# A fused attention and soft mixture of experts on one core: other positions of all tasks, buffers given to expert tiles step by step, and the end laid out anew

## The chip, the core and the metric

The kernel runs on one core of a Trainium2 chip. The time is that of the device in microseconds for one execution; the median of several executions is given. Five engines work side by side, each on its own list of instructions: the tensor engine (PE, with its weight loads as PEld), the vector engine (DVE), the scalar engine (ACT), GpSimd (POOL) and SyncE (SP), which issues nearly all transfers.

## The reference

Attention over 8 images, 8 heads, 576 positions and 64 dimensions, then a soft mixture of 8 experts with 4 slots each (32 slots) over all 4608 rows of 512 features:

```python
q_rot, k_rot = rotate(q), rotate(k)
scores = scale * q_rot @ k_rot.T
attn = softmax(scores, -1)                 # per head, 576 x 576
x = (attn @ v).transpose(0, 2, 1, 3).reshape(4608, 512)
logits = x @ phi                           # 4608 x 32
d = softmax(logits, 0)                     # dispatch: over all rows
slot_input = (d.T @ x).reshape(8, 4, 512)
for e in range(8):
    slot_out[e] = relu(slot_input[e] @ w1[e]) @ w2[e]     # 512 -> 1024 -> 512
c = softmax(logits, 1)                     # combine: over the slots
out = c @ slot_out
```

## The kernel before

**Pairs.** Two heads of an image are a pair; there are 32 (NPAIR), four to an image. For each pair some forty small tasks run: load0 and load1 (q and k come in, two buffers x_in), spin0 and spin1 (rotation products on POOL), join (sum on DVE), high (float16 high half on ACT) and low (the rest, DVE), which together fill a buffer hl of the pool stk, four of them; eight tasks m00 to m31 and m_rem (scores once, in high halves, for each column's maximum, read by DVE from PSUM); m_min, m_turn, m_half and m_rows (the maxima are reduced, transposed, scaled, and sent by two small transfers into one of two tiles called peak); t0 to t8 (scores in three products and the peaks as a fourth, exponential by ACT into a_t, for t8 into a_rem); av0 to av8 (times v, all into one PSUM tile o_ps); o_out (ACT copies o_ps out in two pieces), recip, norm (POOL), natural (transpose on PE), natural_out (ACT), logits and logits_sum.

**Images.** After an image's last pair come stat0, stat1, slots (running maximum and sums over the rows, with rescaling) and soft0 to soft3 (softmax over the slots, the combine weights cn_sb).

**The order.** PE, ACT and DVE run in the order in which the program writes its tasks; SP and POOL too until the last pair is through. That order is the table WHEN (for pairs 0 to 4 the table FIRST): each task has a position in quarter pairs, to which 4 is added per pair, and `line` is all of them sorted (L590, run at L619). PSUM has three two-bank tiles (bank2, L210) for all tasks but av, which take turns.

**Expert weights.** They are 64 tiles of 512 KB. The first 26 (N_W) are loaded in the course of the pairs into the pool wp (task weights). When the last low is done, the input buffers are closed (release_io) and 7 tiles go there, one per task trickle0 to trickle3; after the last t8 the four hl buffers are closed (release_stk) for 4 more; after the last av8 those of attention (release_att) for one. Two (N_WB) come when the normed outputs xn are read, 7 (N_LEAD) and the remaining 17 when expert products have read the tiles of wp. SP issues them in this order.

**The end** (L627 to L835). Norm, transpose, logits and statistics of the last pair; the slot sums of the last image (mains, L670) and their rescaling (L695 to L714); the experts' first layer in four groups (ffn1, L720), each followed by a transpose (ffn1_turn); the second layer in 16 steps for each half of the features (ffn2_steps); gather; and nine combine tasks for each half, each with an output of 512 KB (L767). The second half's second layer is interleaved with the first half's combine. The combine weights are split in a high and low part (c_split), transposed on PE (c_tr) and copied out (c_evac), for two images at a time: turn 0 between the slot sums and their rescaling (L685), turn 1 after the first ffn1 (L793), turn 2 after the fourth, turn 3 in the first half's combine. An output is staged in one of seven tiles that held weights.

Of the kernel before, what the change touches and what calls it, by code (L numbers as in the profile page):

```python
# [28 lines left out]
N_W = 26  # L29
N_WA = 5  # L30
N_WB = 2
N_WE = 3
N_WL = 1
N_X = 4
N_CS = 1
N_CE = 2
C_POOL = 4
LATE = (0, 2)
N_LEAD = 7
TURNS = (0, 0, 1, 0, 0, 0)  # L40
LEAD_STEPS = 2
STEPS = (1, 2, 2, 2, 2, 2, 2, 2, 1)
N_WARM = 23
N_HEAT = 12
N_CST = 4 - N_CE
# [13 lines left out]
    "m_min": (-2.33553, -2.33553, -3.36903, -2.33553), "m_turn": (-1.87097, -1.91584, -1.95052, -1.87097),  # L59
    "m_half": (-1.83711, -1.83711, -1.79, -1.83711), "m_rows": (-0.49269, -0.26643, -0.62853, -0.47686),  # L60
# [56 lines left out]
def attn_softmoe(ctx, tc, qk, v, phi, w, cs, ident, sel, seg, out):  # L117
# [50 lines left out]

    loaded = {}
    halves = {}  # L170
    c_tiles = []
# [636 lines left out]
    for k in range(16):  # L808
# [3 lines left out]
        if k == 8:  # L812
            c_turns(TURNS[3])
# [77 lines left out]
```

## Time and profile before

| | us |
|---|---|
| median of 3 runs | 552.83 (552.35 to 553.71) |
| the profiled execution | 551.77 |
| its span, from the first to the last instruction | 550.0 |
| PE busy in it | 516.9 |
| DVE, ACT, POOL busy | 374.6, 308.5, 287.4 |
| mean granted clock of PE, share of 2.4 GHz | 0.974 |

The profile is of one execution. Busy times of PE include the modelled ends of pipelined matmuls. In a chain of waits each piece is what released the next, followed back from the last instruction; in a timeline each line is a run of like instructions, with its start, its length and, in brackets, the idle time before it.

### The profile page before, as it was taken

What the parts mean: (1) busy time and instruction counts of PE and PEld (TensorE: products, weight loads), DVE (VectorE), ACT (ScalarE), POOL (GpSimd) and SP (SyncE); (2) the same over time, 40 slices, a digit from 0 to 9 for tenths busy, and PEclk for the clock granted to TensorE, in tenths of its full rate; (3) what the DMA queues carried; (4) which work ended last, traced back from release to release, by engine and by line L of the source; (5) the groups of instructions that cost most, each with busy time, mean ns of one, the idle gap of its engine ahead of it and who ended that gap; (6) DMA issues with size and microseconds to landing.
All of it is one profiled execution on the core that took longest, in us unless ns stands there. A gap on an engine that the chain in (4) does not pass through costs nothing.

```text
span 550.0 us, 24116 instructions
## 1 busy us (share of the span) xinstructions
PE 516.9 (94%) x10824; PEld 388.4 (71%) x10824; DVE 374.6 (68%) x591; ACT 308.5 (56%) x615; POOL 287.4 (52%) x338
## 2 busy tenths in 40 slices
PE   4599999999999999999999999999999999799992
PEld 2277777777777777777777777777777777553551
DVE  6788768778777878787778777877887651222162
ACT  2156564766665666566656666566666656334442
POOL 3965678756665666565656766665767011110000
PEclk9699999999999999999999999999999999969997
DMA  7631554444435443544444353434343155349998
GB/s 244 199 125 35 198 190 151 134 145 160 148 108 190 151 143 123 183 158 114 150 151 167 100 179 107 170 119 159 125 151 114 34 212 203 107 133 398 409 415 330
DMA packets 28487, 93.92 MB, mean 171 GB/s; under 512 B 4064, under 2 KB 5856, under 8 KB 28384
## 3 DMA queue, kind: packets, MB, share of 16 engines
q1 hardware_dynamic: 28370, 92.37, 48.1%
q8 instruction: 85, 1.39, 1.0%
q14 instruction: 18, 0.15, 0.1%
q10 hardware_dynamic: 14, 0.00, 0.0%
HBM read 82.85 MB, written 9.44 MB: 168 GB/s over the span
## 4 chain that ended last, share of the span: by engine, by line
PE 83%; DVE 6%; DMA 5%; ACT 2%; issue 1%; SPq 0%; ACTq 0%; DVEq 0%
PE o_ps L303 27%; PE s_ps L268 22%; PE s_ps L221 9%; PE s_ps L350 4%; PE o_ps L310 4%; DMA w_exp<-in_w 3%; PE s_ps L229 2%; PE s_ps L272 2%; PE s_ps L724 2%; PE s_ps L410 1%; PE t_ps L775 1%; DVE nm L223 1%; PE s_ps L360 1%; PE s_ps L242 1%; DMA x_in<-in_qk 1%
## 5 line engine op out<-in xcount | busy, mean ns | idle before, releaser
L187 POOL TENSOR_TENSOR x_in<-x_in,cs_sb 128x288 f32<-128x288 f32 x248 | 221.8, 929 | 78.7 <-DMA x_in<-in_qk 65.9
L223 DVE TENSOR_REDUCE nm<-s_ps 128x2 f32<-128x576 f32 x256 | 188.3, 755 | 79.0 <-PE s_ps L221 74.8
L283 ACT ACTIVATE a_t<-s_ps 128x576 f32<-128x576 f32 x256 | 152.8, 653 | 126.1 <-PE s_ps L268 123.3
L303 PE MATMUL o_ps<-v_in,a_t 128*64 128x65 f32 x4608 | 164.5, 225 | 0.3 <-ACT o_sb L324 0.2
L303 PEld LDWEIGHTS o_ps<-v_in,a_t 128*64 128x64 f32 x4608 | 145.8, 138 | 25.3 <-issue 17.4
L268 PE MATMUL s_ps<-hl 64*128 64x288 f16 x1536 | 134.4, 283 | 0.6 <-DVE nm L231 0.3
L334 POOL TENSOR_TENSOR xn<-o_sb,rr 128x512 f32<-128x512 f32 x31 | 44.4, 1432 | 95.8 <-DVE rr L330 85.4
L268 PEld LDWEIGHTS <-hl 64*128 64x128 f16 x1536 | 76.1, 94 | 19.8 <-issue 2.3
L221 PE MATMUL s_ps<-hl 64*128 64x288 f16 x512 | 73.9, 291 | 3.6 <-DVE l_sb L372 1.4
L268 PE MATMUL s_ps<-peak,lift 64*128 64x288 f16 x512 | 74.5, 283 | 0.0
L191 DVE TENSOR_TENSOR x_in<-x_in 128x1152 f32<-128x1152 f32 (+1 forms) x35 | 50.8, 1451 | 0.1
L196 ACT CAST hl<-x_in 128x576 f16<-128x576 f32 (+1 forms) x66 | 40.6, 651 | 17.8 <-DVE x_in L191 17.7
L200 DVE TENSOR_TENSOR hl<-x_in,hl 128x1152 f16<-128x1152 f32 x32 | 43.3, 1355 | 0.4 <-ACT hl L196 0.4
L221 PEld LDWEIGHTS <-hl 64*128 64x128 f16 x512 | 28.0, 93 | 20.3 <-issue 4.1
L283 ACT ACTIVATE a_rem<-s_ps 128x640 f32<-128x640 f32 x32 | 22.5, 703 | 32.0 <-PE s_ps L274 31.9
L231 DVE TENSOR_REDUCE nm<-s_ps 128x2 f32<-128x576 f32 x32 | 24.2, 755 | 8.8 <-PE s_ps L229 8.8
L268 PEld LDWEIGHTS <-lift 64*128 64x128 f16 x512 | 26.2, 94 | 5.4
L350 PE MATMUL s_ps<-id_sb,xn 128*128 128x128 f32 (+1 forms) x160 | 26.7, 279 | 1.2 <-DVE xn L334 1.1
L350 PEld LDWEIGHTS s_ps<-id_sb,xn 128*128 128x128 f32 (+1 forms) x160 | 17.8, 140 | 13.7 <-issue 13.4
L310 PEld LDWEIGHTS o_ps<-v_in,a_rem 64*64 64x64 f32 x1152 | 22.1, 134 | 6.3 <-issue 5.7
L310 PE MATMUL o_ps<-v_in,a_rem 64*64 64x65 f32 x1152 | 26.5, 224 | 0.0
L323 ACT COPY o_sb<-o_ps 128x585 f32<-128x585 f32 x31 | 20.1, 647 | 5.7 <-PE o_ps L310 2.7
(172 smaller groups left out, 521.8 us busy)
## 6 DMA issues: line engine op xcount, KB each, us to landing
x_in<-in_qk SPq DMA_DIRECT2D x62, 576.0 KB
w_exp<-in_w SPq DMA_DIRECT2D x63, 512.0 KB
v_in<-in_v SPq DMA_DIRECT2D x32, 325.0 KB
out<-w_exp SPq DMA_DIRECT2D x18, 512.0 KB
x_in<-in_qk SPq DMA_DIRECT2D x4, 288.0 KB
cs_sb<-in_cs SPq DMA_DIRECT2D x2, 288.0 KB
wk<-in_w SPq DMA_DIRECT2D x1, 512.0 KB
peak<-mr SPq DMA_DIRECT2D x31, 2.0 KB
```

The source lines that it names most:

```text
L187: eng.tensor_tensor(out=x[:, :, c], in0=x[:, :, c], in1=cs_sb[:, :, c], op=ALU.mult)
L191: nc.vector.tensor_tensor(out=x[:, t, 0, c], in0=x[:, t, 0, c], in1=x[:, t, 1, c], op=ALU.add)
L196: nc.scalar.copy(out=halves[p][:, 1 + t, c], in_=loaded[p][:, t, 0, c])
L200: nc.vector.tensor_tensor(out=hl[:, 0:4:3], in0=x[:, :, 0], in1=hl[:, 1:3], op=ALU.subtract)
L221: nc.tensor.matmul(s[:, h, 0:HC], lhsT=hl[rows[h], QH, P * j:P * j + P], rhs=hl[rows[h], KH, half[n]], start=True, stop=True)
L223: nc.vector.tensor_reduce(out=maxima(p)[:, n, j:8:4], in_=s[:, :, 0:HC], axis=AX.X, op=ALU.max, negate=True)
L268: nc.tensor.matmul(s[:, h, 0:HC], lhsT=lhs, rhs=rhs[:, half[n]], start=first, stop=last)
L283: nc.scalar.activation(out=a, in_=s, func=AF.Exp, scale=SCALE)
L303: nc.tensor.matmul(o, lhsT=ats[p, i][:, h, D * t:D * t + D], rhs=vts[p][:, u], start=(i == 0 and j == 0), stop=False)
L310: nc.tensor.matmul(o, lhsT=rems[p][r, at:at + D], rhs=vts[p][r, KB - 1 + h], start=False, stop=(j == (4 if c == h else 3)))
L334: eng.tensor_tensor(out=x[:, 0:4].rearrange("p j h d -> p h j d"), in0=o[:, 1:9, 0:D].rearrange("p (h j) d -> p h j d", h=2), in1=rr[:, 1: ...
L350: nc.tensor.transpose(t[:, P * j:min(P * j + P, S)], xns[p][r, j], id_sb[r, r])
```

## The change

WHEN and FIRST are new throughout. Besides, in the pairs:

- t8 stands behind t0, and a_rem has two buffers. m_rows, m_turn and load_v stand earlier in relation to the t tasks; low of pair 0 stands ahead of its maxima. The 12 warming matmuls (heat) run ahead of pair 0's m_turn and not behind it.
- o_out's second copy is a task of its own, o_down. The sums zacc are rescaled by ACT. The softmax over slots reads PSUM directly and no longer through copies of ACT.
- stk has three single buffers (N_HL), given back one by one after the scores of pairs 29, 30 and 31. The peaks lie in att, o_sb in late.
- 29 tiles are loaded in wp, 5 in wx, one in each of the three released hl buffers, one after att, three after late (release_late, after the last logits), then 2, 7 and the remaining 14.

At the end turn 0 stands behind the last norm and ahead of natural, its split is made during the pairs; turn 1 behind natural, in o_ps; turn 2 ahead of the third ffn1; turn 3 ahead of the first gather. PSUM has four one-bank tiles t_ps, two a_ps and one d_ps of two banks for the turns. Outputs are staged in eight tiles. The first half's combine runs two by two with four steps of the second layer between.

```diff
-N_W = 26
+N_W = 29
-N_WE = 3
+N_WH = (1, 1)
+N_WV = 3
+N_CST = 2
+WK = 6
-N_CS = 1
-N_CE = 2
+N_CS = 2
-LATE = (0, 2)
+EVACS = {0: 1, 1: 2, 2: 1, 3: 2}
-TURNS = (0, 0, 1, 0, 0, 0)
+STAGE = (("wx", 5),) * 5 + (("wv", 3),) * 3
+SPLIT_AT = ("av1", 31)
-STEPS = (1, 2, 2, 2, 2, 2, 2, 2, 1)
+STEPS = (0, 4, 0, 4, 0, 4, 0, 2, 0)
...
-    "t0": (0.33666, 0.34281, 0.33666, 0.34817), "trickle0": 0.4431, "load_v": (0.46244, 0.46244, 0.46244, 1.17098),
...
-    "trickle2": 2.5296, "trickle3": 3.4658, "t8": 4.1742, "av6": (4.18738, 4.18738, 4.18738, 4.2365),
...
+    "t0": (0.03408, 0.04023, 0.03408, 0.04559), "t8": 0.07615, "trickle0": 0.4431, "t1": 0.50424,
...
+    "t5": (0.68207, 0.68207, 0.68207, 0.67267), "av0": (0.75615, 0.79604, 0.75615, 0.75615),
...
-    stk = early.enter_context(tc.tile_pool(name="stk", bufs=4))
+    early = [ctx.enter_context(ExitStack()) for _ in range(N_HL)]
+    stk = [early[i].enter_context(tc.tile_pool(name=f"stk{i}", bufs=1)) for i in range(N_HL)]
...
-            rems[p] = a = att.tile([P, 10 * D], F32, name="a_rem")
+            rems[p] = a = att.tile([P, 10 * D], F32, name="a_rem", bufs=2)
...
-            nc.vector.scalar_tensor_tensor(out=zacc, in0=zacc, scalar=al, in1=sd, op0=ALU.mult, op1=ALU.add)
+            for c in range(2):
+                nc.scalar.activation(out=zacc[:, c:c + 1], in_=zacc[:, c:c + 1], func=AF.Identity, scale=al,
+                                     bias=sd[:, c:c + 1])
...
+    def c_split(q, pool=None):
+        csps[q] = csp = (pool.tile([P, 2, 5, 2, NS], F32R, name="a_rem", bufs=2) if pool else
+                         hold["cp"].tile([P, 2, 5, 2, NS], F32R, name="csp", bufs=N_CS))
...
+    def release_stk(i):
+        while later:
+            trickle(0)
+        early[i].close()
+        if i == N_HL - 1:
+            load_w(grow("wk", 1), 1, n=WK)
+        else:
+            grow(f"wh{i}", N_WH[i])
+            for _ in range(N_WH[i]):
+                load_w(hold[f"wh{i}"], N_WH[i])
...
+    def release_late():
+        vals.close()
+        grow("wv", N_WV)
+        for _ in range(N_WV):
+            load_w(hold["wv"], N_WV)
...
-        "m_turn": lambda p: (m_turn(p), p == 0 and heat(N_HEAT)),
+        "m_turn": lambda p: (p == 0 and heat(N_HEAT), m_turn(p)),
...
-    release_att()
-    c_split(0)
+    ac, vc = nc.scalar.copy, nc.vector.tensor_copy
     recip(p)
     norm(p, nc.vector, True)
+    c_tr(0, bank2())
+    release_att()
+    c_split(1)
     natural(p)
     natural_out(p)
+    c_tr(1, o_ps)
+    evac = c_evac(0, (vc, ac))
+    list(evac)
     logits(p)
...
-    vals.close()
+    release_late()
     banks.close()
...
     nc.scalar.activation(out=e, in_=e, func=AF.Exp)
+    list(c_evac(1, (ac, ac)))
+    c_split(2)
...
     mains(1)
-    c_tr(0)
-    c_split(1)
-    list(c_evac(0))
...
     prev = (0, 0, ffn1(0, 0))
-    c_turn(1)
...
-            list(c_soft_tasks(B - 1, ps_t.tile([P, 512], F32, name="t_ps")))
-            while len(w_tiles) < 8 * E:
+            list(c_soft_tasks(B - 1, bank()))
+            c_tr(2)
+            c_split(3)
+            while order:
                 load_w(wp, N_W)
+            list(c_evac(2, (ac, ac)))
...
-    c_turns(TURNS[4])
+    c_tr(3)
     sl0 = gather(0, sos[0])
```

## Rows read from the trace of the kernel before

**Rows 1.** The page: PE's busy time, its forty slices in tenths, the transfers' GB/s.

```profile
PE 516.9 (94%) x10824; PEld 388.4 (71%) x10824; DVE 374.6 (68%) x591; ACT 308.5 (56%) x615; POOL 287.4 (52%) x338
...
PE   4599999999999999999999999999999999799992
...
GB/s 244 199 125 35 198 190 151 134 145 160 148 108 190 151 143 123 183 158 114 150 151 167 100 179 107 170 119 159 125 151 114 34 212 203 107 133 398 409 415 330
```

**Rows 2.** Windows: length, busy PE, PEld, DVE, ACT, POOL, granted clock, DMA share, GB/s.

```profile
320.00:360.00 40.00, 39.41 (x908) 30.92 (x900) 32.18 (x53) 24.05 (x50) 23.89 (x29) 1.00 0.46 157
```

**Rows 3.** The chain that ended last, 476 to 498: start, length, what.

```profile
476.80 0.84 PE s_ps L350 x5
...
478.36 0.43 PE s_ps L360 x8
...
481.54 1.01 PE t_ps L673 x16
482.55 0.58 PE t_ps L682 x8
...
484.14 1.47 PE s_ps L454 x6
...
485.88 0.59 PE o_ps L698 x2
486.46 1.56 PE o_ps L703 x8
...
488.40 4.98 PE s_ps L724 x32
493.37 0.81 PE s_ps L454 x6
...
494.20 3.65 PE s_ps L724 x32
```

**Rows 4.** Windows where PE's clock falls and comes back; columns as in rows 2.

```profile
478.00:480.00 2.00, 0.54 (x16) 0.38 (x16) 0.93 (x3) 0.31 (x2) 0.00 (x0) 1.00 0.00 0
...
480.50:481.00 0.50, 0.33 (x1) 0.14 (x1) 0.09 (x1) 0.50 (x3) 0.22 (x1) 0.91 0.00 0
...
491.00:491.50 0.50, 0.50 (x12) 0.17 (x8) 0.00 (x0) 0.00 (x0) 0.00 (x0) 0.85 0.00 0
```

**Rows 5.** Window of the transfers at their full rate; columns as in rows 2.

```profile
500.00:502.00 2.00, 2.00 (x24) 0.41 (x15) 1.01 (x4) 0.34 (x1) 0.00 (x0) 1.00 1.04 426
```

**Rows 6.** Timeline of PE and SP: both gathers, the second half's first combine and output.

```profile
515.31 1.41 PE L761 MATMUL s_ps<-so,seg_sb 128*128 128x256 f32 x4
...
531.37 0.82 PE L761 MATMUL s_ps<-so,seg_sb 128*128 128x256 f32 x4
532.65 0.98 PE L775 MATMUL t_ps<-kl,cst 128*128 128x256 f32 x6 [0.46 <-ACT kl L764]
...
534.19 0.33 SPq L778 DMA_DIRECT2D out<-w_exp  x1
```

**Rows 7.** The chain in the start-up: low of pair 0, m_turn, first scores.

```profile
13.96 1.83 DVE hl L200
...
21.36 0.37 PE s_ps L242
...
26.08 1.08 PE s_ps L268 x8
```

**Rows 8.** Change of pair: chain on PE (two t, then four), timeline of ACT.

```profile
302.31 0.98 PE s_ps L268 x16
...
310.12 2.06 PE s_ps L268 x32
...
310.81 2.28 ACT L283 ACTIVATE a_t<-s_ps 128x576 f32<-128x576 f32 x4
```

**Rows 9.** Timeline: the transfer of a pair's maxima, and the matmuls that use them.

```profile
305.00 0.52 SPq L251 DMA_DIRECT2D peak<-mr  x1
...
308.74 0.29 PE L268 MATMUL s_ps<-peak,lift 64*128 64x288 f16 x2
```

More of the change, by code (lines that the diff above doesn't have):

```diff
@@ L154, in attn_softmoe @@
         nc.vector.memset(lift[64 * h:64 * h + 1], CM)
-    peaks = [const.tile([P, S], F16, name=f"peak{i}") for i in range(2)]
+    peaks = [att.tile([P, S], F16, name=f"peak{i}") for i in range(2)]
     for t in peaks:
@@ L289, in attn_softmoe @@
     O_AT = 512 - NJ * VC
-    o_sbs = [const.tile([P, 2 * NJ, VC], F32, name=f"o_sb{i}") for i in range(2)]
+    o_sbs = [late.tile([P, 2 * NJ, VC], F32, name=f"o_sb{i}", bufs=1) for i in range(2)]
     for t in o_sbs:
@@ L453, in c_tr, with c_evac @@
                 w = P if j < 4 else 64
-                nc.tensor.transpose(turning[q][0:w, b, 64 * j:64 * j + P],
+                nc.tensor.transpose(t[0:w, b, 64 * j:64 * j + P],
                                     csp[:, b, j:min(j + 2, 5)].rearrange("p j a n -> p (j a n)").bitcast(F32), id_sb)
-    def c_evac(q, both=False):
-        cst, crt, _ = c_tiles[0]
+    def c_evac(q, copies):
         t = turning.pop(q)
-        copies = (nc.scalar.copy, nc.vector.tensor_copy)
+        cst.append(hold["cp"].tile([P, 2, 4, P], F32R, name=f"cst{q}") if q < N_CST else
+                   wp.tile([P, 2, 4, P], F32R, name="w_exp", bufs=N_W))
         for d in range(2):
             dst = slice(64 * d, 64 * d + 64)
-            copy = copies[d * both]
+            copy = copies[d]
             for s in range(2):
@@ L494, in release_io @@
-        extra.extend((wx, wa))
-        later.extend([(wa, N_CST)] * N_CST + [(wx, N_WA)] * N_WA)
+        grow("wx", N_WA)
+        later.extend(["wx"] * N_WA)
     def trickle(p):
         if later:
-            load_w(*later.pop(0))
-    def release_stk():
-        early.close()
-        hx = ctx.enter_context(tc.tile_pool(name="hx", bufs=1, side="right", reuse_waits="tile"))
-        extra.append(hx)
-        load_w(hx, 1, "wk")
-        we = ctx.enter_context(tc.tile_pool(name="we", bufs=N_WE, side="right", reuse_waits="tile"))
-        for _ in range(N_WE):
-            load_w(we, N_WE)
+            load_w(hold[later.pop(0)], N_WA)
@@ L618, in attn_softmoe @@
     nc.sync.dma_start(out=sel_sb, in_=sel)
+    held = N_HL
     for when, name, p in line:
         do(name, p)
-        if not extra and ("low", NPAIR - 1) in done:
+        if "wx" not in hold and ("low", NPAIR - 1) in done:
             release_io()
-        if (name, p) == (f"t{KB - 1}", NPAIR - 1):
-            while later:
-                trickle(p)
-            release_stk()
+        if held and "wx" in hold and all((f"t{b}", NPAIR - held) in done for b in range(KB)):
+            held -= 1
+            release_stk(held)
+        if not csps and all(x in done for x in (("av8", NPAIR - 2), ("t8", NPAIR - 1), SPLIT_AT)):
+            c_split(0, att)
     p = NPAIR - 1
     steady.close()
-    release_att()
-    c_split(0)
+    ac, vc = nc.scalar.copy, nc.vector.tensor_copy
     recip(p)
     norm(p, nc.vector, True)
+    c_tr(0, bank2())
+    release_att()
+    c_split(1)
     natural(p)
     natural_out(p)
+    c_tr(1, o_ps)
+    evac = c_evac(0, (vc, ac))
+    list(evac)
     logits(p)
@@ L707, in attn_softmoe @@
     tail = ctx.enter_context(tc.tile_pool(name="tail", bufs=1, reuse_waits="tile"))
-    wb = ctx.enter_context(tc.tile_pool(name="wb", bufs=1, reuse_waits="tile"))
-    for i in range(N_WB):
-        load_w(wb, 1, f"w_exp{i}")
+    wb = ctx.enter_context(tc.tile_pool(name="wb", bufs=N_WB, reuse_waits="tile"))
+    for _ in range(N_WB):
+        load_w(wb, N_WB)
     for _ in range(N_LEAD):
```

236 lines of the change are left out of this document (105 added, 131 removed), and 47 rows, old and new, of tables (FIRST, WHEN).

## The prediction

> **What bounds the kernel now.** Read first the page's engine table and its forty slices [rows 1]: the tensor engine is busy for 516.9 of 550.0 us, and its tenths are at 9 from the third slice almost to the last. Only the first two slices and the last ones have holes, so only these, and what the tensor engine does in each task, can give or take much. One window of the middle [rows 2] says the same more sharply: 39.41 of 40 us, in one of the leakiest windows of the steady part; over the whole of it the idle time adds up to a few us. The order of the 32 pairs could at best win that.
>
> Read next the chain that ended last, from the end of the last pair's attention to the first expert layer [rows 3]. The transpose of the last pair starts at 476.80, the first matmuls of the experts at 488.40. In between the tensor engine takes turns with the vector and scalar engines, and one piece of the chain has nothing to do with it: the 1.47 us of L454, which turns combine weights (c_tr) between the slot sums and their rescaling. A second turn (0.81 us) stands between the first two expert products. Then the granted clock [rows 4]: from 478 to 480 the tensor engine worked 0.54 of 2 us; at about 480.9 the clock fell from 2.4 to 1.2 GHz and came back at about 491.2. Everything in the chain between cost twice: the first expert product 4.98 us, the same work next 3.65.
>
> Last, the transfers. They stand still from 478 to 480 [rows 4], since buffers are not yet free, and from 493 on they are full to the end [rows 5], at some 410 GB/s. A tile of weights or output has 0.524 MB, so 1.28 us. After the first expert product 24 weight tiles (7 of N_LEAD, then the last 17) and 18 outputs are left: 42 x 1.28 = 53.8 us from 493 gives 546.8, and the page's last slices show them full that far [rows 1]. So is this the bound? Only jointly. The first output of the second half is issued at 534.19 [rows 6]; nine outputs of 1.28 are 11.5, and with some 1.3 us until the first of them flows this gives 547.0. Both bounds meet within 0.3 us. The end moves only if both move: fewer weight tiles late, and an earlier start of the second half's combine, which is at 532.65 [rows 6]. From there to the end of the span are 17.35 us that the change leaves as they are.
>
> **The change part by part.** The sum is made against the profiled execution, 551.77 us with a span of 550.0; the median of the three runs is 552.83, and I carry the difference over to it unchanged.
>
> *Weight tiles.* Loaded before the first expert product is done: now 26 + 2 + 5 + 1 + 3 + 1 + 2 = 40, then 29 + 5 + 1 + 1 + 1 + 1 + 3 + 2 = 43. Three tiles fewer are left: 3 x 1.28 = 3.8 us less for the transfer bound. The three of N_WV load when the last pair's logits have read their buffers, at about 479, where the transfers now stand still; the two of N_WB, behind them on SyncE's queue, wait for the slot sums as before, so nothing is held back. By this the transfer bound lies at least as far down as the tensor engine's path gets (they start some 4.5 us behind the first expert product, by the terms below at 489.2 at the latest; 39 tiles x 1.28 = 49.9 gives 539.1, ahead of 547.0 - 6.4 = 540.6). The part buys nothing by itself; it lets the other parts count. The Trainium skill (DMA: Bandwidth & Descriptors, Specifications) puts the memory's limit for a core at some 358 GB/s; by that a tile would take an estimated 1.46 us. The trace disagrees: 426 GB/s in one window, some 410 over the tail.
>
> *Combine weights turned elsewhere.* c_tr(0) goes into the wait for the last norm, c_tr(1) into the wait for the scalar engine's copy behind the transpose, both with their inputs ready early. The 1.47 us leave the chain. c_tr(1) runs 0.81 from the end of the transpose (476.80 + 0.84) and ends at 478.45, the logits start at 478.36 now [rows 3]: +0.15 with the issue. The 0.81 after the first expert product go: -0.81. The evacuations of both move to vector and scalar engines that wait there for the tensor engine; if that cover were gone they would stand before logits_sum, and the copies of one half on one engine are what it would cost, under 2 us. The third turn stays before the experts' second group. The fourth leaves the combine phase and covers the gather: now L761 takes 1.41 from its start, and at the second gather, where its input is there, 0.82 [rows 6], so -0.6. Sum with the clock as now: -1.47 + 0.15 - 0.81 - 0.6 = -2.7; if the slow stretch stays as long as it is and other work slides into it, the first turn is worth 0.81 and not 1.47, and the sum is -2.1.
>
> *The clock.* The two turns put 1.6 us of transposes where the engine was idle for most of 475.7 to 480. If the clock then stays at 2.4 GHz, L673 twice (1.01 each), L682 (0.58), L698 (0.59) and L703 (1.56) take half: 4.75 / 2 = -2.4, and I count no more for the smaller ones, since the vector engine's updates fill that. The first expert product takes 3.65: -1.3. Together -3.7. Bounds: 0 if nothing changes, and above 0 if the clock falls later, over dense work (rival 2).
>
> *Start-up.* The low halves of pair 0 come ahead of its maxima on the vector engine, and the 12 warming matmuls ahead of m_turn. Now [rows 7]: low takes 1.83, m_turn stands at 21.36 with the warming behind it, the first scores at 26.08. Then: low can't start before the last cast, the maxima, the first of which now runs ahead of that, wait for it, and m_turn slips by an estimated 0.7 us to 22.1, with the warming done before it. Five maxima of pair 1 fill the time until the peaks land, t8 comes first. What is lost at m_turn is in part given back, since more work is done when the scores start. From -1.0 to +1.0; I take 0.
>
> *Steady pairs.* All tasks of a pair stay, t8 goes from the end of a pair to behind t0 (hence two buffers of a_rem), and t1 to t5 follow each other at the change of pair, where it was t1 to t4. Now the four take 2.06 us on the tensor engine and 2.28 on the scalar engine [rows 8]: the scalar engine is the slower, and the tensor engine runs 0.1 us behind its own pace (two of them take 0.98 where nothing holds it). A fifth adds 2.28 / 4 - 0.49 = 0.08, but m31 now stands ahead of them and gives the scalar engine 0.2 us to copy o_ps first. Net 0, from -0.1 to +0.35 a pair. m_rows: its DMA is issued at 305.00 and the peaks are used at 308.74 without a wait [rows 9], so 3.7 us are enough; in the new order the transpose, two maxima, two av tasks, the logits and one maximum lie between, some 4.4 us. SyncE passes load_v and weights ahead of it; these wait for nothing later than m_turn's maxima, so the row transfer isn't held. The change of zacc to the scalar engine, softmax reading PSUM directly and the moved peaks and o_sb are off the tensor engine: 0. Three hl buffers for four: the first cast into one follows the last read of it in the order, 0. For all this 0, from -2.5 (the idle time of the middle gone) to +2.5. The three single buffers of hl given to expert tiles load five tiles and one more around pair 29's scores; the transfers are mostly idle there.
>
> **How the numbers follow.** Main case: clock kept, -2.7 - 3.7 = -6.4: the second half's combine starts at 526.2, span 543.6, and on the median 552.83 - 6.4 = 546.4 us. Measurement tells from no change about 0.3%, 1.7 us here.
>
> **Rivals.** *1. The clock falls all the same,* at about the same time and for as long. Then -2.1: 550.7. For it: after the logits the engine still waits for a sum, a maximum, a bias and an exponential, and the present stretch at 1.2 GHz held on for 10 us although the chain is nearly all tensor engine there [rows 3, 4]. Against it: the wait that went before is more than half filled. The Trainium skill (TensorE: Matmul & The Clock Gate, A second HAM failure mode) says that short idle times between groups of matmuls alone can bring the clock down and up; by that rule this rival is what comes, at the 550.7 worked out above. In this trace the clock held through the steady part's short gaps, and fell only after 478 to 480 with 0.54 of 2 us [rows 2, 4]; neither case settles it.
>
> *2. It falls later,* in the rescaling, and the same 10.3 us at half speed lie over dense expert products, so 5.1 us are lost. -6.4 + 5.1 = -1.3: 551.5.
>
> *3. The scalar engine becomes the bound at each change of pair.* Five exponentials behind the two copies of o_ps: if m31's maximum is late on the vector engine, the third buffer isn't free, and the tensor engine waits 0.35 us a pair. From 6.4 / 28 = 0.23 us a pair on, the gain is gone. 28 x 0.35 = +9.8, with the main gain 556.2: slower. Against it: m31's maximum is the second in a row on the vector engine there, with nothing longer ahead of it.
>
> *4. Nothing but the three tiles counts:* the turns displace other work as long as they are. Then the tensor engine's bound stays: 552.8.
>
> **Chances.** Main case 0.48, rival 1 0.20, rival 2 0.12, rival 3 0.12, rival 4 and others 0.08. The clock kept is the likeliest, since the idle time it fell after is what the change fills. The range: main case with the start and the steady part from -2.4 to the other cases, 544.0 to 553.0; this leaves out rival 3 and a bit on either side. The main case's own range is 544.0 to 549.0. Faster by over 0.3%: nearly all of the main case, two thirds of rival 1 and some of 2: 0.69. Within 0.3%: the rest of 1 and 2, and 4: 0.16. Slower: 0.15.
>
> **What would show it.** Right: no row of L454's successor between the slot sums and the rescaling; two turns between 475.7 and 478.5; a granted clock of 1.00 from there through the first expert product, which then takes 3.65 us; transfers busy at 480 to 484; the second half's first output issued some 6 us earlier, and the span ending as far behind it as now. Wrong: a clock of 0.50 over expert products (rivals 1, 2); idle time of the tensor engine ahead of t4 or t5 put down to the scalar or vector engine, in pair after pair (rival 3); a wait for a weight tile in the second expert layer; scores of pair 0 starting after 27.5.

## The result and the profile after

The changed kernel takes 534.13 us (median of 4 runs, 531.43 to 534.23) where the kernel before took 552.59 beside it: a ratio of 0.966, 95% interval 0.9615 to 0.9705. In a later series it took 536.89 (e15 below: 535.44 to 537.83, ratio 0.977, 0.974 to 0.979); where these 2.8 us come from is told there. The direction of the prediction was right. The size was not: 546.4 was forecast, and 544.0 was the lowest time that it allowed for.

Lines of the profile page of after (span; busy time of the engines; forty slices of PE in tenths):

```profile
span 532.2 us, 24086 instructions
...
PE 506.0 (95%) x10824; PEld 386.3 (73%) x10824; DVE 359.8 (68%) x580; ACT 308.3 (58%) x618; POOL 250.5 (47%) x330
...
PE   4799999999999999999999999999999999989991
```

The same 10,824 matmuls take 10.9 us less of PE's "busy" time [rows 1], although the slices are at 9 as before. That is the first sign: the gain is inside what the profile calls busy.

**Where the 17.8 us of span went**, by the starts of matmuls in both traces. The slot sums of the first image start at 103.28 instead of 105.54 (-2.3). From there to the last matmul of attention it is 359.1 instead of 369.9 (-10.8). But in the new order the slot sums stand later among the tasks: 1,852 matmuls have started ahead of them, 1,792 before. So the cut has to be made at one and the same task. The av_rem of pair 5, the first pair that runs by WHEN, starts at 107.53 instead of 111.77 (-4.2): the start-up and the first pairs, forecast at 0. From there to the av_rem of the last pair, 26 pairs later, it is 354.3 instead of 363.1 (-8.8): the steady part, forecast at 0. From the last matmul of attention to the end of the span it is 69.8 instead of 74.5 (-4.8): the tail, forecast at -6.4. The first and the last of these differ between profiles of after itself: in e15 below they are -2.6 and -3.3, the steady part is -8.0.

**The steady part.** The window that rows 2 show of before, in after:

```profile
320.00:360.00 40.00, 39.88 (x932) 31.74 (x928) 29.52 (x47) 25.87 (x51) 22.66 (x31) 1.00 0.39 140
```

Before, 908 matmuls stood in this window with PE 98.5% busy; now 932 do, with 99.7%. The busy share rose by 1.2%, the matmuls by 2.6%. Over 16 whole pairs, from av_rem to av_rem (before, then after), it is plainer still:

```profile
209.41:435.49 226.08, 224.51 (x5139) 176.48 (x5137) 174.94 (x269) 139.93 (x280) 140.16 (x159) 1.00 0.42 138
```

```profile
202.94:423.47 220.53, 219.99 (x5147) 175.19 (x5139) 164.16 (x260) 141.12 (x285) 114.36 (x153) 1.00 0.41 146
```

The pairs took 5.55 us less, and only 1.0 of that is idle time of PE. So most of the gain can't be seen in idle time. To see it one has to look at when one matmul starts after another. The chain of one pair without an image's end (start, length, what) in before:

```profile
303.29 0.80 PE s_ps L350 x5
304.09 0.21 PE s_ps L242
...
306.87 0.23 PE s_ps L229 x4
...
309.14 0.74 PE o_ps L310 x36
309.89 0.23 PE s_ps L221 x2
```

and the same view of after:

```profile
300.19 0.09 PE s_ps L237
300.27 0.06 PE o_ps L318
...
300.42 0.57 PE o_ps L318 x30
...
301.22 2.62 PE s_ps L276 x40
...
309.12 0.21 PE s_ps L250
309.33 0.64 PE s_ps L361 x5
309.97 0.24 PE s_ps L229 x4
```

Two things are to be seen. m_rem (L229 before, L237 after) and av_rem (L310, L318) run through each other in 0.80 us, where they took 0.23 + 0.74. And natural (L350, L361) with m_turn (L242, L250) takes 0.21 + 0.64, where it took 0.80 + 0.21. The pair takes 13.18 us instead of 13.51. What sets these lengths is in the shapes of the matmuls; groups of PE in after by form (the two numbers with a star: the rows and columns of the array that the weights take):

```profile
L311 PE MATMUL o_ps<-v_in,a_t 128*64 128x65 f32 x146 | 5.4, 225 | 0.0
...
L229 PE MATMUL s_ps<-hl 64*128 64x288 f16 x17 | 2.2, 287 | 0.0
L318 PE MATMUL o_ps<-v_in,a_rem 64*64 64x65 f32 x36 | 1.0, 223 | 0.0
...
L361 PE MATMUL s_ps<-id_sb,xn 128*128 128x128 f32 x4 | 0.6, 272 | 0.0
...
L237 PE MATMUL s_ps<-hl 64*64 64x288 f16 x4 | 0.4, 282 | 0.0
```

From the start of one matmul to the start of the next, in the steady part of the two traces (typical values; two numbers where places or traces differ):

```
same part of the array            next on another part
av to av          128x64     30   av to m         128x64 to 64x128    154
m to its second   64x128      4   m to av         64x128 to 128x64    213
m to m or t       64x128    130   t to natural    64x128 to 128x128   252
av_rem to av_rem  64x64   17-19   natural to m_turn                   202
m_rem and av_rem  64x64    7-47   m_turn to av                        208
natural to m      64x128      5   m to av_rem     64x128 to 64x64     213
m_turn to natural           113   logits to m     128x32 to 64x128  152-237
                                  av to logits    128x64 to 128x32    152
(ns)
```

In all of these a matmul that takes another part of the array than the one ahead of it starts 150 to 250 ns behind it. Over 16 pairs of each trace there are 15.75 such changes a pair before (3.06 us from start to start in them) and 12.75 after (2.38 us). Half of the 0.68 us that this frees is given back, since maxima and scores that stood behind another part now stand behind each other, at some 130 ns of their own. The other 0.34 us a pair remain (14.13 to 13.79): over the 26 pairs, the 8.8 us of the steady part. The Trainium skill states such a cost (TensorEngine Tiling (Array Packing), Key Properties: "Changing tiling mode (not just tile) drains the TensorE"). This trace agrees: 150 to 250 ns at each change. m_turn, of 9 columns, stands to natural's first matmuls on 128x128 as to its own kind (113 ns; among themselves 109 to 118). Natural's last one is on 64x128, so m_turn behind natural is a change (202) and a maximum behind it is none (5).

**The tail.** Timeline of PE in after, from the last av_rem on (in brackets, the idle time ahead and what ended it):

```profile
461.84 0.81 PE L318 MATMUL o_ps<-v_in,a_rem 64*64 64x65 f32 x36
462.58 0.87 PE L469 MATMUL s_ps<-id_sb,a_rem 128*128 128x128 f32 x6
...
464.61 0.87 PE L469 MATMUL o_ps<-id_sb,csp 128*128 128x128 f32 x6
...
467.21 0.29 PE L688 MATMUL t_ps<-id_sb,m_run 128*128 128x128 f32 x1 [1.21 <-DVE m_run L393]
467.97 0.33 PE L689 MATMUL t_ps<-id_sb,d_t 128*128 128x128 f32 x1 [0.47 <-ACT d_t L394]
...
473.77 4.60 PE L749 MATMUL a_ps<-w_exp,slot_t 128*32 128x512 f32 x28 [0.38 <-DVE slot_t L739]
```

The two turns (L469) stand where they were forecast, and the first expert product starts 11.3 us behind attention instead of 12.9. But behind the last logits the engine still waits 1.21 and 0.47 us, and the clock still falls (windows of after, columns as in rows 2):

```profile
466.00:468.00 2.00, 0.33 (x3) 0.16 (x2) 0.93 (x3) 1.95 (x6) 0.00 (x0) 1.00 0.93 344
...
470.00:472.00 2.00, 2.00 (x23) 1.62 (x13) 1.84 (x7) 1.97 (x4) 0.13 (x1) 0.50 0.65 209
...
476.00:478.00 2.00, 2.00 (x20) 0.56 (x16) 0.00 (x0) 0.00 (x0) 0.00 (x0) 0.84 0.00 0
```

It is at 1.2 GHz from about 469.9 to 476.7, 6.8 us instead of 10.3 [rows 4]; in e15's profile of the same kernel it is 10.2. Later, between the two gathers, the timeline of after shows:

```profile
503.17 1.93 PE L769 MATMUL a_ps<-w_exp 128*32 128x256 f32 x32
505.03 1.21 PE L795 MATMUL t_ps<-sl,cst 128*128 128x256 f32 x8
```

and that of before at the same place:

```profile
519.54 0.74 PE L775 MATMUL t_ps<-sl,cst 128*128 128x256 f32 x4
520.21 1.07 PE L748 MATMUL o_ps<-w_exp 128*32 128x256 f32 x16
```

From gather to gather it is 13.43 us (500.34 to 513.77) instead of 16.06 (515.31 to 531.37 [rows 6]): 0.75 of it is the fourth turn and 0.64 the stall of the first gather, and some 1.2 are new. The combine's matmuls now come eight at a time between 32 of the second expert layer, not four between sixteen (STEPS in the diff). By the starts, 32 and 8 take 3.00 us now; twice 16 and 4 took 3.34: two changes fewer, between 128x32 and 128x128. No run changes STEPS alone.

### The profile page after: what moved, and what is told of

The parts are those of the page before. It is cut to its first block, busy times and chain, and to the rows that moved or that the text cites. A ratio compares the mean times of both kernels' runs of the same rounds, so it can differ in the third digit from the quotient of the medians.

```text
span 532.2 us, 24086 instructions
## 1 busy us (share of the span) xinstructions
PE 506.0 (95%) x10824; PEld 386.3 (73%) x10824; DVE 359.8 (68%) x580; ACT 308.3 (58%) x618; POOL 250.5 (47%) x330
## 4 chain that ended last, share of the span: by engine, by line
PE 87%; DVE 4%; ACT 4%; DMA 2%; issue 1%; SPq 0%; DVEq 0%; ACTq 0%
PE o_ps L311 27%; PE s_ps L276 24%; PE s_ps L229 8%; PE o_ps L318 4%; PE s_ps L361 3%; PE a_ps L749 3%; PE a_ps L769 3%; PE s_ps L280 2%; PE t_ps L795 2%; PE s_ps L371 2%; DMA x_in<-in_qk 2%; DVE nm L231 1%; PE s_ps L423 1%; PE s_ps L237 1%; PE s_ps L282 1%; PE s_ps L250 1%
## 5 line engine op out<-in xcount | busy, mean ns | idle before, releaser
L231 DVE TENSOR_REDUCE nm<-s_ps 128x2 f32<-128x576 f32 x256 | 184.9, 754 | 63.5 <-PE s_ps L229 61.4
L195 POOL TENSOR_TENSOR x_in<-x_in,cs_sb 128x288 f32<-128x288 f32 x248 | 197.5, 833 | 51.7 <-DMA x_in<-in_qk 41.1
L291 ACT ACTIVATE a_t<-s_ps 128x576 f32<-128x576 f32 x256 | 150.8, 655 | 117.0 <-PE s_ps L276 116.2
L276 PE MATMUL s_ps<-hl 64*128 64x288 f16 x1536 | 134.5, 283 | 0.4 <-DVE nm L231 0.2
L345 POOL TENSOR_TENSOR xn<-o_sb,rr 128x512 f32<-128x512 f32 x31 | 33.4, 1078 | 144.6 <-ACT a_t L291 77.7
L276 PEld LDWEIGHTS <-hl 64*128 64x128 f16 x1536 | 74.4, 94 | 22.4 <-issue 2.8
L229 PE MATMUL s_ps<-hl 64*128 64x288 f16 x512 | 63.4, 289 | 3.0 <-DVE nm L231 1.8
L199 DVE TENSOR_TENSOR x_in<-x_in 128x1152 f32<-128x1152 f32 (+1 forms) x35 | 44.1, 1261 | 0.8 <-POOL x_in L195 0.7
L229 PEld LDWEIGHTS <-hl 64*128 64x128 f16 x512 | 24.7, 96 | 18.3 <-issue 6.3
L239 DVE TENSOR_REDUCE nm<-s_ps 128x2 f32<-128x576 f32 x32 | 24.3, 758 | 16.6 <-PE s_ps L237 16.6
L365 ACT COPY xt<-s_ps 128x576 f32<-128x576 f32 x32 | 20.3, 635 | 17.8 <-PE s_ps L361 17.5
L318 PE MATMUL o_ps<-v_in,a_rem 64*64 64x65 f32 x1152 | 30.5, 223 | 0.0
L318 PEld LDWEIGHTS o_ps<-v_in,a_rem 64*64 64x64 f32 x1152 | 26.4, 133 | 0.4 <-issue 0.2
L361 PE MATMUL s_ps<-id_sb,xn 128*128 128x128 f32 (+1 forms) x160 | 25.9, 274 | 0.4 <-DVE xn L345 0.4
L361 PEld LDWEIGHTS s_ps<-id_sb,xn 128*128 128x128 f32 (+1 forms) x160 | 19.1, 140 | 6.8 <-issue 5.7
```

Of the source, the lines that this page charges most:

```text
L195: eng.tensor_tensor(out=x[:, :, c], in0=x[:, :, c], in1=cs_sb[:, :, c], op=ALU.mult)
L199: nc.vector.tensor_tensor(out=x[:, t, 0, c], in0=x[:, t, 0, c], in1=x[:, t, 1, c], op=ALU.add)
L229: nc.tensor.matmul(s[:, h, 0:HC], lhsT=hl[rows[h], QH, P * j:P * j + P], rhs=hl[rows[h], KH, half[n]], start=True, stop=True)
L231: nc.vector.tensor_reduce(out=maxima(p)[:, n, j:8:4], in_=s[:, :, 0:HC], axis=AX.X, op=ALU.max, negate=True)
L276: nc.tensor.matmul(s[:, h, 0:HC], lhsT=lhs, rhs=rhs[:, half[n]], start=first, stop=last)
L291: nc.scalar.activation(out=a, in_=s, func=AF.Exp, scale=SCALE)
```

## The experiments

Each ratio is to the kernel before as it ran in the same series. There it took from 549.1 to 552.6 us, so times from different series can differ by some 3 us for that alone.

**1. The order alone, in before.** The tables WHEN and FIRST of after, two buffers of a_rem, the warming ahead of m_turn, and the hl buffers closed behind the last t7, which now comes last; everything else as before.

```diff
-WHEN = {... before ...}; FIRST = {...}
+WHEN = {... after ...}; FIRST = {...}          # o_down left out: o_out copies both as before
-            rems[p] = a = att.tile([P, 10 * D], F32, name="a_rem")
+            rems[p] = a = att.tile([P, 10 * D], F32, name="a_rem", bufs=2)
```

> The kernel before with the positions of all tasks of the changed one (both tables), two buffers of a_rem and the warming ahead of m_turn; its own buffers for weights and its own end. Theory A, the order alone shortens what the tensor engine does, since it changes less often between kinds of matmul: a steady pair takes 13.18 us instead of 13.51, the start-up gives 2 us, so about 552.6 - 10.5 - 2 = 540 us. Theory B, the gain is at the end (tiles loaded early, turns moved) and the order gives no more than the idle time of the middle, 2.5 us: 550 us or more.

Measured 544.17 us (ratio 0.988, 0.982 to 0.993): 6.6 less than before beside it (550.76), half of the 12.5 that theory A expected. The trace shows why. Pairs without an image's end take 13.18 us, as in after. The pair behind each image's last takes, from m_turn to m_turn, 14.5 to 15.1 in five of six images (14.0 in the first) where after has 13.5. The chain in such a pair of e1:

```profile
232.54 0.32 DVE cm L428
...
232.88 0.87 DVE ln L429
233.76 0.68 DVE nm L223
...
234.48 0.29 PE s_ps L229 x2
```

The softmax of the combine weights (L428, L429, with two copies and a zero fill ahead) stands on the vector engine ahead of a maximum (nm), and m_rem waits for the buffer that this maximum reads. The steps L433 to L436 do the same again to m_turn later in the pair. So a part of the change that the prediction put at 0, "softmax reading PSUM directly", was next.

**2. The order and the softmax, in before.** e1 with the function c_soft_tasks of after.

```diff
+        nc.vector.tensor_reduce(out=cm, in_=tl, axis=AX.X, op=ALU.max)
+        nc.vector.tensor_tensor(out=ln, in0=tl, in1=cm.unsqueeze(2).broadcast_to([P, 5, NS]), op=ALU.subtract)
...
+        nc.scalar.activation(out=cz, in_=cz, func=AF.Identity, bias=eps)
+        yield
```

> The kernel before with the positions of all tasks from the kernel after (as e1_order_in_before) and, beside that, the new steps of the softmax over a token's slots (read from PSUM directly, its last four vector steps spread over two tasks, one on the scalar engine). e1 took 544.17 us; its trace shows pairs of 13.2 us as in the kernel after, but at each change of image a pair of 14.5 to 15.1 us where the kernel after has 13.5, with the vector engine working off the softmax ahead of the maxima. Theory A (the order and the softmax belong together): these pairs go to 13.5, some 1.1 us less for each of six images, so 537 to 538 us. Theory B (the softmax steps are off the path, as the prediction had it): 544 us.

Measured 537.79 us (0.979, 0.976 to 0.983). The pairs of 14.5 to 15.1 us are 13.5, and the last matmul of attention stands at 460.8, even earlier than in after (462.4). Order and softmax are the whole of the steady part; what after has beyond this kernel is its tail, 69.8 us where e6 has 75.7. Some of these 5.9 are the clock: e6's tail has 13.7 us at 1.2 GHz, after's 6.8.

**3. The old softmax, in after.** The other way round.

```diff
+        ln = small.tile([P, 5, NS], F32, name="ln", bufs=1)
+        nc.gpsimd.memset(ln[64:P, 4, :], 0.0)
+        nc.scalar.copy(out=ln[:, 0:4, :], in_=tp[:, 0:P].rearrange("p (j n) -> p j n", n=NS))
...
-            copy(out=hold["crt"][dst, 2 * q:2 * q + 2, :], in_=t[0:64, :, 320:384])
+            copy(out=hold["crt"][dst, 2 * q:2 * q + 2, :], in_=t[0:64, :, 256:320])
```

> The kernel after with the softmax over a token's slots as before (two copies and a zero fill into SBUF, then four vector steps in one task); nothing else is changed but the columns that the combine weights of the last 64 tokens are read from. Theory A (in the new order these steps stand on the vector engine ahead of the maxima and the transpose m_turn, as in e1_order_in_before): the pair at a change of image takes 14.5 to 15.1 us instead of 13.5, six or seven times, so 6.5 to 9 us slower than the kernel after of the same call. Theory B (only in the frame of before): as the kernel after.

Measured 541.75 us (0.985, 0.982 to 0.988) beside 536.89 of after in the same series (e15): 4.9 more by the medians, less than theory A's 6.5 to 9. In the trace the pairs at the changes of image take 14.4 to 15.05 us in five of six images, as in e1, and attention ends 5.7 us later than in e15; 1.4 of that come back since e15's tail had a longer stretch at 1.2 GHz. The place is the one that theory A named, the size some 5 us.

**4. m_rem beside av_rem, in before.** One number of the order.

```diff
-    "m_rem": -3.82562
+    "m_rem": -3.6410
```

> The kernel before with one task moved: m_rem stands right ahead of av8 (both 64 x 64 in the array), where m00 stood. Theory A: the change from m_rem to av (0.21 us from start to start) and that from m00 to av8 (0.21) become one of t8 to av and one of some 0.01, so 0.2 us a pair, 28 pairs: 552.6 - 5.6 = 547 us. Theory B, what counts is when PSUM's readers are through, not what stands beside what: 552.6, no change.

Measured 553.17 us (1.006, 1.003 to 1.009): a miss of theory A. The 0.17 us are there: m_rem and av8 take 0.92 us together instead of 1.09. But the chain shows a new wait ahead of them:

```profile
252.38 0.25 PE s_ps L221 x2
...
252.65 0.77 DVE nm L223
...
253.46 0.29 PE s_ps L229 x2
```

m_rem comes right behind a maximum and needs the buffer that an earlier one still holds; m to m_rem is 525 ns, where m to av_rem was 213. And t8, behind which m_rem stood at 32 ns, now has an av of another part behind it, at 146. The gain of 0.17 is paid with 0.31 and 0.11, and the pair grows from 13.51 to 13.79. Attention ends 3.4 us later; 2.8 of that come back in the tail, where the clock was at 1.2 GHz for 6.8 us and not for 10.2.

**5. The same with the maximum behind, in before.**

```diff
-    "m_rem": -3.82562 ... "m00": (-3.64252, -3.64252, -3.64252, -3.64223)
+    "m_rem": -3.6410 ... "m00": (-3.6, -3.6, -3.6, -3.6)
```

> The kernel before with m_rem right ahead of av8 and m00 behind av8 instead of ahead of it. e2_rem_by_rem_in_before had m_rem and av8 together but m00 right ahead of them; there m_rem and av8 took 0.92 us instead of 1.09, and m_rem waited 0.31 us longer for its PSUM buffer. Here the maxima lie apart from m_rem. Theory A (m_rem and av_rem, both on 64x64, run through each other; e2's loss was the buffer): 0.17 us less a pair, 546 to 548 us against a kernel before at 551 to 552.6. Theory B (nothing is to be had from it): 551 us or more.

Measured 559.15 us (1.018, 1.013 to 1.022), a miss and worse. m_rem and av_rem again take 0.92 us, but now the two maxima behind them and the first score wait: t1 to t4 take 2.45 us instead of 2.10, the chain has 0.77 us of the vector engine's nm between them, and the pair takes 13.92. With three buffers and 0.75 us for each maximum on the vector engine, neither of these two places pays. In after, t0 and t8 stand between the last maximum and m_rem; that its gain rests on the early t8 is argued, no run moves t8 alone.

**6. One m between two av, in after.** m00 from beside m21 to between av0 and av1.

```diff
-    "m00": (-6.86772, -6.86772, -6.86772, -6.86743)
+    "m00": (-7.20741, -7.20898, -7.20898, -7.16909)
```

> The changed kernel with one task moved in the steady part: m00 stands between av0 and av1 instead of behind both. All else is as it was, the vector engine has time to read it. Theory A: two more changes a pair (av to m 0.154, m to av 0.213) for 0.118 and 0.033 without them, +0.22 us a pair, 27 pairs: 534.1 + 5.8 = 540 us. Theory B: nothing waits for it, 534.1.

Measured 556.48 us (1.010, 1.006 to 1.014), some 20 us slower than after (attention ends 20.6 us later in the trace): far more than either theory. In a plain pair av0, m00 and av1 take 1.68 us where av0 and av1 with m00 at its pace among other maxima took 1.32: 0.36 us for two changes more. But the pair grows by 0.70. On the vector engine the following stands behind m00 now:

```profile
259.49 0.76 DVE L231 TENSOR_REDUCE nm<-s_ps 128x2 f32<-128x576 f32 x1 [1.56 <-PE s_ps L229]
260.16 1.35 DVE L199 TENSOR_TENSOR x_in<-x_in 128x1152 f32<-128x1152 f32 x1
...
261.55 1.36 DVE L231 TENSOR_REDUCE nm<-s_ps 128x2 f32<-128x576 f32 x2
```

The two maxima that stand behind av1 are reduced only behind the 1.35 us of x_in, and t6 and t7, which need their buffers, take 1.32 us instead of 0.99. At the ends of images the pairs grow by up to 1.3 us; there the scores wait for a_t and for their peaks, up to 0.8 us. So this run shows the price of a change, but more than half of its loss is something else.

**7. natural ahead of m_turn, in after.**

```diff
-    "natural": (6.70186, 6.65236, 6.60514, 6.72707)
+    "natural": (6.41, 6.33, 6.33, 6.41)
```

> The kernel after with natural ahead of m_turn instead of behind it, nothing else. Theory A (what costs time is each change of the part of the array that a matmul takes, rows x columns): natural ends on 64x128, as the maxima behind it, so that this change is free now (5 ns from start to start); with m_turn (128x9) between them there is one change more: 202 + some 230 ns instead of 114 + 5, so some 0.3 us a pair over 28 to 31 pairs: 542.5 to 543.5 us from 534.1. Theory B (the gain of the kernel after comes from waits that went, not from what follows what): 534 to 535 us.

Measured 541.68 us (0.985, 0.981 to 0.990). It looks like a hit of theory A, but the trace takes half of that back: with these numbers natural is ahead in two pairs of four only. In a plain pair of that kind natural, m_turn and the two maxima behind take 0.56 us more:

```profile
243.73 0.86 PE L361 MATMUL s_ps<-id_sb,xn 128*128 128x128 f32 x5
244.52 0.28 PE L250 MATMUL s_ps<-id_sb,nm 128*9 128x128 f32 x1
244.73 0.72 PE L229 MATMUL s_ps<-hl 64*128 64x288 f16 x4
```

Of these 0.29 are changes (natural to m_turn 201 and m_turn to m 210 instead of 114 and 5 ns), as expected for one pair; by the reading of experiment 8 they are two, not the one of the text on record. Another 0.2 are a wait of the second maximum for its buffer. The price is confirmed, the total only by accident.

**8. logits beside m_turn, in after.**

```diff
-    "logits": (7.35988, 7.35988, 7.32871, 7.35629)
+    "logits": (10.5, 10.5, 10.5, 7.35629)
```

> The kernel after with the logits of three pairs in four (not the last of an image) moved to right behind the next m_turn: both take columns of 32 or fewer. Theory A (each change of the part of the array costs): now av to logits 152 and logits to m 236 ns, then av to m 154 and m_turn to logits some 30, so two changes and 0.2 us less in three pairs of four, some 23 pairs: 529 to 530.5 us from 534.1. Theory B: no change, 534 us, or slower if m_turn's rows or the one buffer of xt come late.

Measured 541.94 us (0.987, 0.982 to 0.992): a miss. m_turn to logits is 208 ns, not 30: with its 9 columns m_turn counts as 128x128. So nothing was saved, and the next maximum now comes 0.55 us earlier than the cast on the scalar engine that it reads. Pairs took 13.8 us instead of 13.2.

**9. The turns back, and the tiles late, in after.** e4 puts the first two turns where before had them, their splits at the end of attention. e5 loads the three wv tiles behind the seven lead tiles.

```diff
-    c_tr(0, bank2())
     release_att()
...
     mains(1)
+    c_tr(0)
+    list(c_evac(0, (ac, ac)))
```

```diff
         grow("wv", N_WV)
-        for _ in range(N_WV):
-            load_w(hold["wv"], N_WV)
...
     for _ in range(N_LEAD):
         load_w(wp, N_W)
+    for _ in range(N_WV):
+        load_w(hold["wv"], N_WV)
```

> The changed kernel with the first two turns of the combine weights where they stood before: turn 0 behind the slot sums, turn 1 behind the first expert product, both splits at the end of attention. By the terms of the prediction +2.1 to +2.7, and the clock, whose stretch at half speed is 6.8 us with the turns in the gap and was 10.2 without, costs up to 1.7 more: 536.2 to 538.5. If the turns only displace other work: 534.1.

> The kernel after with the three wv tiles loaded behind the seven lead tiles instead of at the last pair's logits: the same transfers, three tiles later. In the trace of after the transfers are full (408 to 411 GB/s) from about 478 to 529.5, three us ahead of the end of the span. Theory A (the transfers set the end of the kernel after): three tiles of 1.28 us more in that stretch, 537 to 538 us from 534.1. Theory B (the tensor engine's path sets it, the tiles buy nothing by themselves): 534 us.

e4: 535.38 us (0.974, 0.969 to 0.979), between the two medians of after (534.13 and 536.89). In its trace the first expert product starts 12.2 us behind attention instead of 11.3, and the second gather 0.64 us later. e5: 536.58 us, but from 531.2 to 538.57 (0.973, 0.967 to 0.980), again between them; by its trace theory B holds. Its tail takes 71.4 us; that of e15, with the clock at 1.2 GHz for the same 10.2 us, takes 71.2, so the three tiles cost some 0.2 and not 3.8. The transfers have holes near the end, where after's have nearly none (windows, columns as in rows 2; after, then e5):

```profile
510.00:520.00 10.00, 9.50 (x84) 6.67 (x73) 6.77 (x12) 6.02 (x12) 0.00 (x0) 1.00 1.00 397
```

```profile
510.00:520.00 10.00, 9.50 (x90) 6.66 (x90) 6.81 (x13) 5.95 (x12) 0.00 (x0) 1.00 0.94 370
```

With three tiles more to move, the transfers still had room: the tensor engine's path set the end in that run. "The part buys nothing by itself" was right.

**10. The clock and zacc, in after.** e9 adds 20 matmuls of no use in the two waits behind the last logits. e12 puts the rescaling of zacc back on the vector engine. e13 and, in a later series beside after itself (e15), e16 do both.

```diff
+    def keep(o, n):
+        for _ in range(n):
+            nc.tensor.matmul(o[:, 0:P], lhsT=lift, rhs=lift, start=True, stop=True)
...
     logits_sum(p)
+    keep(lt[p][:, 1], 14)
...
     nc.tensor.transpose(mt[:, 0:P], m.broadcast_to([P, P]), id_sb)
+    keep(fp, 6)
```

```diff
-            for c in range(2):
-                nc.scalar.activation(out=zacc[:, c:c + 1], in_=zacc[:, c:c + 1], func=AF.Identity, scale=al,
-                                     bias=sd[:, c:c + 1])
+            nc.vector.scalar_tensor_tensor(out=zacc, in0=zacc, scalar=al, in1=sd, op0=ALU.mult, op1=ALU.add)
```

> The kernel after with 20 matmuls of no use (lift by lift, 128 columns, into free parts of PSUM) in the waits behind the last logits (14 behind the sum of the logits, 6 behind the first transpose of the slot sums), where the tensor engine works 0.33 of 2 us and after which the clock falls (469.9 to 476.7). Theory A (these waits bring the clock down): it stays at 2.4 GHz, the rescaling and the first expert product take 2.4 to 3 us less, the buffers come free and the transfers begin that much earlier: 531 to 532 us from 534.1. Theory B (the clock falls all the same, or what it costs is hidden by the transfers): 534 to 534.5 us.

> The kernel after with the rescaling of zacc on the vector engine again, one instruction, as before. In the trace of after the pair with the slot sums takes 14.98 us; in e6_order_and_softmax_in_before, in the same order, 14.71, and after's scalar engine has the two zacc instructions (0.56 us) ahead of the copies of dn for which the tensor engine waits. Theory A (they are on the path): 0.27 us less for each of seven images, 532.2 us from 534.1. Theory B (off the path, as the prediction had it): 534.1 us.

> Both e9_warm_end and e12_zacc_back in one kernel. If both hold by their theory A, they add: 529 to 530 us; if the clock falls all the same, 532.2 us; if neither, 534 us.

> The kernel after itself, beside the two others on one chip: 531 to 534.3 us.

> The kernel of e13_zacc_back_warm_end, beside the kernel after in one call. If the zacc instructions (0.27 us in each of seven images, 1.9 us) and the clock's fall (2.6 us by the traces of e9 and e13, whose second half's last combine stands 56.2 us behind the attention instead of 58.8) cost what the traces say, it is 4 to 4.5 us faster than the kernel after of this call; if the transfers or the start take it back, less than 1.5 us.

Measured: e9 533.46 us (0.969, 0.965 to 0.973), e12 533.83 (0.970, 0.966 to 0.974), e13 529.88 (0.963, 0.958 to 0.969); later e15 536.89 (0.977, 0.974 to 0.979) and e16 529.11 (0.964, 0.961 to 0.966). The clock in e13, over the same work as the windows of after above:

```profile
465.00:467.00 2.00, 1.46 (x31) 1.22 (x32) 1.32 (x5) 1.49 (x4) 0.00 (x0) 1.00 0.92 371
...
469.00:471.00 2.00, 1.70 (x31) 1.24 (x24) 1.86 (x8) 1.95 (x5) 0.46 (x1) 1.00 0.41 129
...
475.00:477.00 2.00, 2.00 (x24) 0.65 (x20) 0.69 (x1) 0.00 (x0) 0.00 (x0) 1.00 1.00 326
```

It stays at 2.4 GHz, up to behind the second gather and through the first two expert products too, which take 7.07 us from 472.12 on (x64, one row of the timeline) where after takes 8.46. The last matmul of the second gather starts 49.2 us behind attention in e13; in after it is 51.8, in e15 53.1. So the waits did bring the clock down, as theory A has it. The total shows it best between e12 and e13, which ran in one series and differ by the 20 matmuls alone: 533.83 and 529.88 us, with the second gather at 53.3 and 49.2 us behind attention. e9 has 49.25 too, but in the profiled run its start took 1.4 us more than after's and a few pairs up to 0.5 us more, so the total hid most of it. e12 has its pairs with slot sums at 14.71 us instead of 14.98, as theory A has it. The zacc rows of after are

```profile
267.21 0.41 ACT zacc L401 x2
...
267.78 0.26 ACT dn L414
```

and dn is what the tensor engine waits for. In e12 the clock fell for longer in the tail (until about 478), which hid it. Together they give 7.8 us against after in the same series (529.11 to 536.89), more than the 4 to 4.5 expected. The two profiles differ by 8.6 us of span: 4.3 in the tail; 1.9 in the pairs with slot sums, by zacc; 1.3 up to the first slot sums (104.90 to 103.63); the rest, some 1.1, in single pairs of e15 that took 0.1 to 0.4 us longer. e15 had a longer stretch at 1.2 GHz both in the tail and in the start, where its windows stand against those of the first profile of after like this:

```profile
20.00:25.00 5.00, 4.28 (x50) 2.12 (x49) 4.04 (x7) 1.77 (x4) 5.00 (x7) 0.73 0.00 0
25.00:30.00 5.00, 5.00 (x100) 3.88 (x96) 5.00 (x6) 3.61 (x7) 0.88 (x2) 1.00 0.37 102
```

```profile
20.00:25.00 5.00, 4.52 (x42) 2.19 (x40) 4.05 (x7) 1.45 (x3) 5.00 (x7) 0.50 0.00 0
25.00:30.00 5.00, 5.00 (x80) 3.54 (x76) 4.14 (x5) 3.41 (x6) 0.81 (x2) 0.82 0.36 112
```

(after, then e15.) The same kernel, then, gives 1.6 us more or less at the start and 1.5 in the tail, where the clock fell and came back at other times; that is most of the 3.8 us of span between the two profiles of after, and it goes the way of the 2.8 between their medians. e16 beats both kernels.

## Why the prediction was right or wrong

**Steady pairs: wrong, and this is the step that failed.** It held that the order of the pairs "could at best win" the idle time of the middle, -2.5 us. They gave 8.8 (13.79 us a pair for 14.13), of which some 1.7 were idle time. The step took the busy "39.41 of 40 us" for work that can't shrink. But a matmul counts as busy for some 0.28 us, though one of its kind can start 0.13 us or less behind it; so the 0.15 to 0.25 us to a matmul on another part lie under the one ahead and are never idle. e1 and e6 show that order and softmax alone are the gain; the starts over 16 pairs (12.75 changes for 15.75) and e7 show where it lies. The step looked at which tasks a pair has ("all tasks of a pair stay") and at t1 to t5, and was right there: five take 2.62 us, 0.52 each as four did. It did not look at what stands beside natural, m_turn and m_rem.

**Softmax and zacc "off the tensor engine: 0": wrong twice.** The softmax keeps the new order from losing some 5 us (e14 against e15; e1 against e6 has 6.4, of which 1.7 are the difference of before between their series). zacc on the scalar engine costs 0.27 us for each image (e12's pairs).

**Combine weights turned: place right, size off.** The terms were -2.7 with the clock as it was, -2.1 of it for the first two turns. Undoing these (e4) moves the second gather by 0.64 us; the gather's stall went, -0.64 for -0.6 forecast. What came beside it had no term: STEPS, one line of the diff, gives some 1.2 us by the same price of a change, read from the trace alone.

**The clock: the main case was wrong, its reason right.** Rival 1 came nearest: the clock fell, for 6.8 us instead of 10.3 in one profile and for 10.2 in e15's. Rival 2 did not come: the first expert product took 5.03 us (5.47 in e15), 4.98 before. The wait that stayed, 0.33 of 2 us busy behind the last logits, was enough. With that wait filled (e13, e16) the clock is 1.00 from the start-up to behind the second half's gather, and this gather stands 7.1 us nearer to the end of attention than before (its last matmul at 49.2 for 56.35); the forecast for the main case was 6.4, without STEPS. That the tail's -4.8 in after lies not far from the forecast -6.4 is in part luck: the clock's -3.7 did not come, and some 1.2 came that had no term. The Trainium skill (TensorE: Matmul & The Clock Gate, A second HAM failure mode) says that short idle times between groups of matmuls can bring the clock down. e9 and e13 agree: with the waits filled the granted clock read 1.00 where after had 0.50.

**Weight tiles: right that they buy nothing by themselves (e5).** That they were needed to let the other parts count did not show: e5, with as few tiles loaded early as before, kept the gain of the rest.

**Start-up: -4.2 and -2.6 for 0, -1 to +1, up to the av_rem of pair 5: wrong too.** m_turn stands at 21.14, not at 22.1, and the first scores at 23.91 instead of 26.08. The clock is back sooner in one profile (0.73 and 1.00 above, before had 0.50 and 0.81 in these windows), not in the other (0.50 and 0.82). So the 2.6 us that e15 is ahead of before came without the clock, from the start and the order of the first pairs; how the other 1.6 divide between the clock and single pairs stays open.

**Rivals 3 and 4: not seen.** No wait of PE for the scalar engine stands ahead of t4 or t5 in after's pairs.

## What to carry to other kernels

A PE that is 99% busy can still lose a few per cent: count, task by task, how often neighbouring matmuls take different rows x columns of the array, and price each change from starts (here 0.15 to 0.25 us where a matmul of the same kind follows at 0.005 to 0.13). Then check for each task that is moved which buffer it needs and who on the vector engine still holds it; three of the moves tried here (e2, e3, e8) lost time to that. A wait of about one microsecond can come ahead of 7 to 10 us at half the clock, as behind the last logits here.

## What the runs showed of the hardware

- A change of the array part costs 150 to 250 ns from start to start: 154 from 128x64 to 64x128, 213 back, 152 to 252 around 128x128, against 4 to 130 ns within one part (165 between the two transposes of d_t). Between matmuls on 64x64 that take different quarters (m_rem and av_rem) there is no such price (7 to 47 ns on average), though one is in fp16 and the other in fp32: they ran through each other.
- A transposing matmul with 9 columns behaved as one on 128x128 (113 ns to natural), not as one on 128x32 (208 ns to the logits in e11).
- 20 small matmuls without a use, some 1.2 us of the engine's time in which it waited anyway, were worth 2.6 us and more of the tail: with them the clock did not fall there (e12 to e13: 3.95 us in the time).
- Moved alone, e2, e8 and e11 made the kernel that they changed slower, though each moved only one or two tasks of a pair.
